# Head of an attention and mixing kernel: first third of q and k by halves of the heads, another load order, deeper load gates, a new order of operations with less padding

## The chip, the cores and the metric

The kernel runs on one core of one Trainium2 chip. The metric is the device time of one execution in microseconds (us), lower is better. The profile shows the core's span from first to last instruction, about 1.8 us shorter than the device time. The granted clock of TensorE is a share of full speed; it is 1.000 in the profiled run of the kernel before.

## The reference, cut to what matters

```python
# attention: q, k, v are [4, 8, 768, 64]; a token sees the first 8 tokens and the 96 before it
scores = scale * q @ k.T + bias                  # bias by head and distance
a = softmax(where(keep, scores, -1e9))
x = (a @ v), heads side by side                  # [4, 768, 512]
# then a mixing block
theta = x @ w_theta
zr, zi = x * cos(theta), x * sin(theta)
y = einsum('ts,bsd->btd', w_tok_r, zr) + einsum('ts,bsd->btd', w_tok_i, zi)
u = x + y
out = u + relu(u @ w_ch)
```

All arrays are float32; the kernel computes in bf16 with float32 accumulation.

## The kernel before

The program is a set of named operations and one list, ORDER, that gives the order in which they are written out. In the traces here each engine takes its own part of that list in order, so an operation that waits holds up those behind it on its engine (in a_256 below PE stands 1.93 us before a transpose, with the data of the scores behind it already there). Names carry batch, third of the sequence (256 tokens), and part: `t0010` transposes a k tile of batch 0 on TensorE (PE), `q000` and `k000` copy the result out of PSUM (the memory that matmuls write to), `kp` and `kg` make a second copy of k whose first 8 columns are the global tokens, `bi` writes the bias, `etab` makes a table of exponentials of it, `s` is one group of score matmuls (two heads), `x` the exponential, `v` the matmul with v, `n` the norm, `xt` the transpose of x (on PE in batches 0 and 1, by DMA in batches 2 and 3), `th` theta, `mx` the mixing, `ch` the last matmul, `load` and `gate` loads on GpSimd (POOL). "+27" behind a name asks for 27 padding matmuls on zeros before it.

```python
ORDER = """
... load4 sid3 etab6 bi0000
cast00/DVE bi0001 bi0010 etab3 load5 t0000 cast10/DVE bi0011 q000/DVE etab1 t0010+5 load6 k000/DVE etab2 kg000
kp000/DVE load7 etab0 cast01/DVE etab5 t0001+27 load8 cast11/DVE etab4 q001/DVE t0011+12 load9 k001/DVE kg001
s000+3 kp001/DVE load10 s001 x0000 x0001 load11 bi0020+3 t0100 ...
"""
```

The head loads q and k of the first 256 tokens of batch 0 as float32 over the queues of SP and ACT, one 128-token tile of all heads at a time, in runs of one token and head (64 floats, 256 B), and casts them on VectorE (DVE):

```python
a = new(st, "e", [T, H, D], FP)
(nc.sync, nc.scalar)[i].dma_start(out=a, in_=(q, k)[i][0, :, t * T:(t + 1) * T, :].rearrange("h p d -> p h d"))
...
vector[o.took](out=tiles[key][:, i, t].rearrange("p (h d) -> p h d", d=D), in_=tiles[st])
```

All other loads go through POOL and cast on the way. A load of number n, from the 20th on, is held by a gate, a one-element copy out of the landing place of load n - DEPTH:

```python
DEPTH = 5
add(f"gate{n}", {"POOL": 0.35},
    lambda: nc.gpsimd.tensor_copy(out=scrap, in_=landed[n - depth]()), ...)
...
ORD = 2     # third(1), v(0,0), v(0,1), third(2), v(0,2), then w_theta
```

The softmax here doesn't subtract the row's maximum and nothing guards it: scores larger than these inputs give would overflow.

Of the kernel before, what the change touches and what calls it, by code (L numbers as in the profile page):

```python
# [9 lines left out]
FP = mybir.dt.float32  # L10
# [27 lines left out]
ones6 hw00 hw10 zero rel ones3 tiny hw01 halfpi hw11 warm0 ones5 ones1 ones4 ones2 load1 ones0 ident sid0 far0  # L38
sid2 far1 load2 dtab0 dtab1 dtab2 load3 dtab3 sid4 sid5 etab7 sid1 sid6 sid7 load4 sid3 etab6 bi0000
cast00/DVE bi0001 bi0010 etab3 load5 t0000 cast10/DVE bi0011 q000/DVE etab1 t0010+5 load6 k000/DVE etab2 kg000  # L40
kp000/DVE load7 etab0 cast01/DVE etab5 t0001+27 load8 cast11/DVE etab4 q001/DVE t0011+12 load9 k001/DVE kg001
s000+3 kp001/DVE load10 s001 x0000 x0001 load11 bi0020+3 t0100 x0010 x0011 bi0021 bi0030 load12 q010/DVE t0110
bi0031 s003 k010/DVE load13 s002 x0030 kg010 kp010/DVE x0031 load14 vpa00/DVE x0020 vpb00/DVE x0021 bi0100+6
load15 v003 v000 v001 load16 bi0101 n000 s010 vpa01/DVE load17 bi0110 x0100 bi0111 vpb01/DVE s011 load18 x0101
n003 bi0120 v002 x0110 load19 n001 bi0121 s012 x0111 n002 bi0130 x0120 v010 bi0131 n010 s013 x0121 v011 x0130
v012 n011 t0200 x0131 n012 t0210 q020/ACT bi0200 k020/DVE xt00 bi0201 xc00/ACT bi0210 kp020/DVE bi0211 kg020
v013 vpa02/DVE s020 n013 s021 x0200 vpb02/DVE xt01+6 x0201 bi0220 gate20 x0210 xc01/DVE bi0221+1 load20 v020
x0211 s022 n020 tw00 gate21 x0220 v021 load21 twc00/DVE bi0230 x0221 bi0231 n021 s023 gate22 th000 x0230
load22 x0231 v022 tw10 ts0 gate23 n022 tw11 load23 v023 twc10/DVE th001 n023 gate24 twc11/ACT load24 tw01 xt02
cos000 twc01/DVE gate25 th011 sin000 load25 xc02/DVE cos001 z000 gate26 th010 load26 sin001 th020 z001 cos010  # L50
gate27 load27 sin010 th021 cos011 z010 gate28 t1000 sin011 load28 tw21 cos020 q100/DVE mx000 gate29 sin020
twc21/DVE load29 t1010 cos021 z011 gate30 mx010 sin021 k100/DVE load30 tx1 vpa10/DVE mx001 gate31 kg100 load31
vpb10/DVE z020 mx011 gate32 kp100/DVE load32 z021 tw20 s100 twc20/DVE s101 gate33 mx002 x1000 load33 x1001
x1010 mx012 u00 x1011 gate34 load34 s102 m101 s103 tw30 u01 x1020 gate35 mx020 x1021 m100 load35 x1030 m102
x1031 mx022 gate36 twc30/DVE load36 m103 mx021 gate37 load37 ut00 u02 ut01 uc00/ACT v102 gate38 t1110 uc01/DVE
load38 tw31 k110/DVE ch01 twc31/ACT gate39 kp110/DVE load39 t1100 kg110 o01 v101 v103 q110/DVE gate40 v100
st01 tw41 load40 ch00 n100 twc41/ACT n101 gate41 ut02 load41 tw40 vpa11/DVE uc02/ACT mx030 o00 twc40/ACT
gate42 vpb11/DVE load42 st00 mx032 n102 n103 mx031 gate43 load43 s110 gate44 u03 s111 load44 x1100 t1200 ch02
x1110 gate45 q120/DVE load45 x1101 ut03 x1111 t1210 m110 gate46 uc03/ACT s112 load46 m111 s113 k120/ACT mx040
o02 gate47 x1120 load47 mx041 kp120/DVE st02 x1121 kg120 gate48 x1130 tw51 m112 load48 v110 twc51/ACT tw50  # L60
n110 v111 mx042 gate49 x1131 n111 load49 twc50/ACT vpa12/DVE s120 u04 s121 gate50 x1200 mx050 load50 m113
x1210 vpb12/DVE ut04 x1201 gate51 ch03 uc04/DVE load51 x1211 m120 s122 o03 gate52 s123 x1220 mx051 load52 m121
x1230 st03 v113 x1221 gate53 xt10 n113 load53 x1231 mx052 m122 ts1 gate54 v120 load54 u05 v112 v121 v122 n112
xc10/ACT ut05 gate55 ch04 n120 load55 uc05/DVE th100 vpa20/DVE gate56 m123 load56 ch05 cos100 vpb20/DVE n121
gate57 sin100 v123 load57 xt11 n122 th101 n123 xc11/ACT gate58 load58 o04 xt12 cos101 o05 th110 st04 gate59
sin101 xc12/DVE load59 st05 th111 cos110 z100 gate60 sin110 th121 z101 load60 cos111 z110 th120 sin111 gate61
vpa21/DVE load61 z111 t2100 cos120 t2010 gate62 vpb21/DVE sin120 load62 t2000 q210/DVE cos121 mx110 z120
gate63 sin121 q200/DVE load63 mx111 k200/ACT z121 gate64 t2110 tx2 load64 kg200 mx112 kp200/DVE k210/DVE
gate65 s200 u11 load65 s201 mx100 x2000 kp210/DVE x2001 ut11 kg210 gate66 x2010 mx101 m200 load66 x2011 s202
m201 gate67 s203 t2200 vpa22/DVE load67 x2020 x2021 t2210 vpb22/DVE x2030 q220/DVE v200 gate68 mx102 x2031  # L70
load68 n200 k220/ACT s210 m203 gate69 s211 m202 load69 x2100 mx120 kp220/DVE x2101 u10 gate70 mx122 x2110
load70 m210 x2111 ut10 s212 kg220 gate71 v202 m211 v201 x2120 load71 ch11 n202 x2121 n201 gate72 v203 s213
load72 n203 mx140 x2130 m212 xt20 gate73 x2131 v210 load73 vpa30/DVE s220 n210 v211 x2200 mx121 gate74 n211
x2201 load74 vpb30/DVE s221 m220 s222 gate75 x2210 ch10 load75 u12 x2211 m213 v220 x2220 ut12 mx130 gate76
x2221 m221 load76 s223 n220 v221 gate77 x2230 m222 mx141 load77 x2231 n221 v222 ts2 gate78 v212 m223 mx131
load78 n212 v223 gate79 n222 v213 load79 mx132 n223 n213 gate80 th200 xt22 load80 o11 mx142 vpa31/DVE cos200
gate81 xt21 u13 load81 sin200 ch12 vpb31/DVE u14 gate82 th201 ut13 load82 o12 mx150 o10 cos201 ut14 z200
sin201 mx151 z201 st12 mx152 st11 th221 st10 u15 t3110 ut15 t3010 k310/DVE t3000 k300/DVE t3100 kp310/ACT
th211 q300/DVE q310/ACT kp300/DVE th210 kg300 kg310 vpa32/DVE th220 cos210 vpb32/DVE sin210 t3210 cos211 t3200
z210 ch13 k320/ACT q320/DVE mx200 sin211 kp320/DVE cos220 o13 ch14 sin220 z211 st13 cos221 mx210 z220 sin221  # L80
o14 mx201 tx3 z221 st14 s300 kg320 s301 mx202 x3000 x3010 mx212 x3001 u20 x3011 m300 s302 ut20 s303 m301 ch15
x3020 x3021 x3030 mx211 o15 x3031 s310 m303 st15 s311 u21 x3100 mx220 x3101 m302 ut21 v300 x3110 mx222 m310
x3111 n300 mx221 m311 v301 u22 v303 v302 v310 n302 ch20 ut22 n301 mx230 o20 n303 ch21 st20 n310 xt30 s312 o21
s313 x3120 mx232 x3121 st21 v311 x3130 mx231 n311 x3131 m312 s320 s321 u23 x3200 mx240 x3201 m313 ut23 v312
x3210 ch22 n312 x3211 m320 s322 s323 o22 x3220 mx241 x3230 m321 st22 v313 x3221 mx250 n313 x3231 m322 ts3 v321
xt31 v320 m323 mx252 n320 v322 v323 n321 ch23 n323 th300 n322 o23 xt32 mx242 cos300 sin300 th301 u24 st23 z300
th310 ut24 cos301 sin301 mx251 cos310 z301 th311 sin310 u25 mx300 z310 cos311 ut25 sin311 th320 z311 th321
cos320 sin320 mx301 cos321 z320 ch24 sin321 z321 mx310 o24 mx302 st24 mx312 u30 mx311 ut30 ch25 u31 mx320 ut31
o25 mx322 st25 mx321 ch30 u32 mx330 ut32 o30 mx331 st30 ch31 mx332 o31 mx340 st31 u33 mx341 ut33 mx342 ch32
u34 mx350 ut34 o32 mx352 st32 mx351 ch33 u35 ut35 o33 ch34 uc35/ACT st33 ch35 o34 ch351 o35 st34 o351 st35  # L90
st351
# [4 lines left out]
def kernel(  # L96
# [13 lines left out]
    nc = tc.nc  # L110
# [51 lines left out]
    DEPTH = 5  # L162
# [58 lines left out]
    def load(fn, us, ndesc, spot, depth=0, reads=(), writes=(), alloc=None):  # L221
        nload[0] += 1
        n = nload[0]
        landed[n] = spot
        after = [f"load{n - 1}"] if n > NFREE else ["hw00"]
        if n == NFREE + 1:
            after = [f"load{i}" for i in range(1, NFREE + 1)]
        if depth:
            add(f"gate{n}", {"POOL": 0.35},
                lambda: nc.gpsimd.tensor_copy(out=scrap, in_=landed[n - depth]()),  # L230
                reads=[("ld", n - depth)], prio=-100 + n - 0.5, after=after)
            after = [f"gate{n}"]
        add(f"load{n}", {"POOL": 0.62 + 0.00028 * ndesc}, fn, reads=reads, writes=list(writes) + [("ld", n)],
            alloc=alloc, prio=-100 + n if n > NFREE else None, lat=(1.05, us + {1: -0.12, 10: 1.1}.get(n, 0.0), 0.65), after=after)
# [39 lines left out]
    def first(i, t):  # L274
# [3 lines left out]
        def fn():  # L278
            a = new(st, "e", [T, H, D], FP)
            (nc.sync, nc.scalar)[i].dma_start(out=a, in_=(q, k)[i][0, :, t * T:(t + 1) * T, :].rearrange("h p d -> p h d"))  # L280

        add(f"hw{i}{t}", {eng: 0.5}, fn, writes=[st], alloc={st: "e"}, prio=-300 + t,
            lat=(0.9, (0.98, 0.7, 1.75, 0.88)[2 * t + i], 1.45), after=["hw00"] if i + t else [])

        def cast():
            if key not in tiles:
                new(key, "qk", [T, 2, 2, DM], BF)
            vector[o.took](out=tiles[key][:, i, t].rearrange("p (h d) -> p h d", d=D), in_=tiles[st])
# [12 lines left out]
    ORD = 2  # L301
# [436 lines left out]
```

## Time and profile before

| | before |
|---|---|
| device time | 174.28 us median of 3 (174.23 to 174.46) |
| span | 172.6 us, clock 1.000 |
| PE busy | 94% |
| first score matmuls | 10.02 us |
| last load issued by POOL | 100.41 us |

How to read it: PE is busy nearly all the time, so what counts is what it is busy with (padding is work of no use) and the few moments in which it waits. A useful mark in the timeline is the load of ACT's sine table, which comes after the last exponential of batch 0. The timeline's columns are start, duration, engine, line, operation and, in brackets, idle time before and what ended it:

```profile
28.30 1.28 ACT L673 ACT_TABLE_LOAD   x1
```

### The profile page before, as it was taken

How to read it: one execution, taken by the hardware profiler on the slowest of the kernel's cores; microseconds unless marked ns; L12 is line 12 of the kernel's file. 1: busy time of each engine (PE TensorE's matmuls, PEld its weight loads, DVE VectorE, ACT ScalarE, POOL GpSimd, SP SyncE). 2: the span in 40 equal slices, each digit the busy share in tenths (PEclk: the TensorE clock that was granted, in tenths of full speed). 3: DMA queues.
4: the chain of work that ended last, by engine and by line, in shares of the span. 5: the costliest groups of instructions: out<-in, count | busy, mean ns of one | idle time of the engine just before them, and what ended most of it. 6: DMA issues, size and time to landing. Idle time of an engine off the chain costs nothing.

```text
span 172.6 us, 4153 instructions
## 1 busy us (share of the span) xinstructions
PE 162.9 (94%) x1598; PEld 93.2 (54%) x1623; DVE 133.4 (77%) x315; ACT 106.0 (61%) x187; POOL 85.0 (49%) x150
## 2 busy tenths in 40 slices
PE   7998999999997999999999997999999999999991
PEld 2764776555664656565555643654555644444440
DVE  7948886798897698999999994795997975634442
ACT  3954988996445888799877540799518847300010
POOL 8998249779895899898996940000000000000000
PEclk9999999999999999999999999999999999999999
DMA  5999999999999999999999999612335364134334
GB/s 121 188 154 155 188 173 123 143 165 163 157 157 178 184 119 158 113 208 129 132 131 114 165 141 177 219 65 77 105 98 139 104 95 123 48 92 133 93 91 182
DMA packets 96868, 23.73 MB, mean 138 GB/s; under 512 B 91088, under 2 KB 93904, under 8 KB 96848
## 3 DMA queue, kind: packets, MB, share of 16 engines
q0 software_dynamic: 73504, 12.33, 100.7%
q1 hardware_dynamic: 21264, 10.62, 25.1%
q10 hardware_dynamic: 2080, 0.52, 1.7%
q8 instruction: 12, 0.20, 0.5%
q14 instruction: 8, 0.07, 0.1%
HBM read 25.69 MB, written 6.29 MB: 185 GB/s over the span
## 4 chain that ended last, share of the span: by engine, by line
PE 48%; DMA 30%; POOL 6%; DVE 6%; issue 5%; ACT 2%; DVEq 0%; POOLq 0%; SPq 0%; ACTq 0%
PE pb L592 22%; DMA qk<-in_k_dram 10%; PE pb L636 9%; PE pa L549 8%; DMA w_theta_bf<-in_moe_w_theta_dram 5%; DMA qk<-in_q_dram 4%; DMA xT<-x 4%; DMA uT<-u 3%; POOL qk L243 3%; DMA w_ch_bf<-in_moe_w_ch_dram 3%; PE pa L451 3%; PE pa L504 3%; PE pb L371 2%; POOL scrap L230 1%; DVE e L482 1%
## 5 line engine op out<-in xcount | busy, mean ns | idle before, releaser
L592 PE MATMUL pb<-zri,w_tokT 128*128 128x512 bf16 x273 | 67.3, 379 | 1.1 <-issue 0.5
L474 ACT ACTIVATE e<-pa 128x512 bf16<-128x512 f32 (+1 forms) x96 | 46.5, 565 | 20.0 <-PE pa L451 19.4
L592 PEld LDWEIGHTS <-w_tokT 128*128 128x128 bf16 x288 | 26.1, 98 | 28.2
L604 DVE TENSOR_TENSOR u<-x,pb 128x512 bf16<-128x512 bf16 x24 | 16.4, 682 | 11.9 <-PE pb L592 11.7
L636 PE MATMUL pb<-w_ch_bf,uT 128*128 128x512 bf16 (+1 forms) x96 | 24.0, 370 | 0.3
L549 PE MATMUL pa<-w_theta_bf,xT 128*128 128x512 bf16 x93 | 22.5, 379 | 1.3 <-DMA xT<-x 1.1
L482 DVE TENSOR_TENSOR e<-e,etab 128x1024 bf16<-128x1024 bf16 (+1 forms) x36 | 22.4, 639 | 0.4
L257 POOL DMA_DIRECT2D vn<-in_v_dram x24 | 21.8, 910 | 1.4 <-issue 1.4
L558 ACT ACTIVATE cs<-pa,halfpi 128x512 bf16<-128x512 f32 x24 | 16.6, 693 | 9.4 <-PE pa L549 9.2
L243 POOL DMA_DIRECT2D qk<-in_q_dram x22 | 19.6, 891 | 1.9 <-issue 0.9
L570 DVE TENSOR_TENSOR zri<-x,cs 128x1024 bf16<-128x1024 bf16 x24 | 16.2, 685 | 5.0 <-ACT cs L560 4.9
L243 POOL DMA_DIRECT2D qk<-in_k_dram x22 | 19.3, 877 | 0.0
L642 DVE SCALAR_TENSOR_TENSOR o<-pb,u 128x512 f32<-128x512 f32 (+1 forms) x25 | 16.2, 663 | 3.7 <-PE pb L636 3.7
L504 PEld LDWEIGHTS <-e 128*128 128x128 bf16 x352 | 14.5, 98 | 5.2
L517 DVE TENSOR_TENSOR x<-pa,rec 128x256 bf16<-128x256 f32 x36 | 15.3, 425 | 1.2
L620 ACT COPY uT<-pb 128x512 bf16<-128x512 bf16 x4 | 2.4, 594 | 20.9 <-PE pb L616 20.9
L549 PEld LDWEIGHTS <-xT 128*128 128x128 bf16 x96 | 8.9, 98 | 11.5 <-DMA xT<-x 1.6
L371 PE MATMUL pb<-ident,qk 128*128 128x128 bf16 x192 | 14.1, 221 | 1.0 <-DMA qk<-in_k_dram 1.0
L451 PEld LDWEIGHTS <-kk 64*128 64x128 bf16 x352 | 9.9, 94 | 9.3 <-issue 8.0
L451 PE MATMUL pa<-qT,kk 64*128 64x128 bf16 x352 | 14.9, 218 | 0.0
L560 ACT ACTIVATE cs<-pa 128x512 bf16<-128x512 f32 x24 | 14.4, 602 | 0.0
L230 POOL COPY scrap<-qk 1x1 bf16<-1x1 bf16 x33 | 11.3, 343 | 5.1 <-DMA qk<-in_k_dram 2.6
(69 smaller groups left out, 207.2 us busy)
## 6 DMA issues: line engine op xcount, KB each, us to landing
out_dram<-o SPq DMA_DIRECT2D x23, 256.0 KB, 2.3
vn<-in_v_dram POOLq DMA_DIRECT2D x24, 128.0 KB, 5.4
qk<-in_q_dram POOLq DMA_DIRECT2D x22, 128.0 KB, 5.5
qk<-in_k_dram POOLq DMA_DIRECT2D x22, 128.0 KB, 5.3
w_nat<-in_moe_w_tok_r_dram POOLq DMA_DIRECT2D x6, 192.0 KB, 6.0
w_nat<-in_moe_w_tok_i_dram POOLq DMA_DIRECT2D x6, 192.0 KB, 6.5
e<-in_k_dram ACTq DMA_DIRECT2D x2, 256.0 KB, 5.8
e<-in_q_dram SPq DMA_DIRECT2D x2, 256.0 KB, 5.1
```

The lines of the kernel that those rows point to most:

```text
L243: nc.gpsimd.dma_start(out=tiles[key][:, i, t].rearrange("p (h d) -> p h d", d=D), in_=(q, k)[i][b, :, r0:r0 + T, :].rearrange("h p d -> p ...
L257: nc.gpsimd.dma_start(out=v_bufs[i][:, t, :, 0:D], in_=v[b, :, r0:r0 + T, :].rearrange("h p d -> p h d"))
L371: nc.tensor.transpose(p_[:, t - u0, p], tiles[key][:, i, t, p * T:(p + 1) * T], ident)
L451: nc.tensor.matmul(p_[hh][:, s], lhsT=tiles["kk", b, kg][R, kt, p, r, :], rhs=tiles["qT", b, g][R, qt, p, :], start=not biased, stop=not b ...
L474: nc.scalar.activation(tiles[ek][:, hh, 0:n], tiles[pb[hh]][:, 0:n], AF.Exp, scale=scale)
L482: nc.vector.tensor_mul(e_[:, :, 0:n], e_[:, :, 0:n], etab[:, 2 * p:2 * p + 2, s0:s0 + n])
L504: nc.tensor.matmul(o, lhsT=l_, rhs=r_, start=(i == 0), stop=(i == len(mms) - 1))
L549: nc.tensor.matmul(p_, lhsT=tiles["xT", b, g][:, p, t, :], rhs=w_theta_bf[:, p, :], start=(p == 0), stop=(p == NP - 1))
L558: nc.scalar.activation(tiles[ck][:, 0], tiles[ps], AF.Sin, bias=halfpi)
L592: nc.tensor.matmul(p_, lhsT=w_tokT[wi][:, 2 * g + t, tt * T:(tt + 1) * T], rhs=tiles["z", b, g][:, t, wi, :], start=(n == 1 and t == 0 and ...
L604: nc.vector.tensor_add(u.rearrange("n (p c) -> n p c", p=NP), tiles["x", b, tt // 2][:, :, tt % 2, :], tiles[ps].rearrange("n (p c) -> n p ...
L636: nc.tensor.matmul(p_, lhsT=tiles["uT", b, tt][:, p, :], rhs=w_ch_bf[:, p, i * w:(i + 1) * w], start=(p == 0), stop=(p == NP - 1))
```

## The change

Its intent is to start the scores earlier and to hold PE up less. The transfers of the head bring four heads of both tiles instead of eight heads of one, in runs of two tokens (512 B), so that two of the four score groups can start after half the data. The later copy out of PSUM undoes the token order. Third 2 of q and k is loaded ahead of v of the middle third, and w_theta ahead of v of the last third. The gates are set to 8 loads in the first part and 6 later. The whole list of operations was ordered anew, with 24 padding matmuls where there were 63.

```diff
-    DEPTH = 5
+    DEPTH = 6
+    DEPTH1 = 8
...
-            a = new(st, "e", [T, H, D], FP)
-            (nc.sync, nc.scalar)[i].dma_start(out=a, in_=(q, k)[i][0, :, t * T:(t + 1) * T, :].rearrange("h p d -> p h d"))
+            a = new(st, "e", [T, H // 2, 2 * D], FP)
+            (nc.sync, nc.scalar)[i].dma_start(
+                out=a, in_=(q, k)[i][0, H // 2 * t:H // 2 * (t + 1), 0:2 * T, :].rearrange("h (p j) d -> p h (j d)", j=2))
...
+        third(1), load_v(0, 0), third(2), load_v(0, 1), load_w("w_theta", ...), load_v(0, 2)
...
+                vector[o.took](out=d_.rearrange("c t p (n j) -> c t p n j", j=2),
+                               in_=tiles[ps].rearrange("c p j (t n) -> c t p n j", t=2))
...
-kp000/DVE load7 etab0 cast01/DVE etab5 t0001+27 load8 cast11/DVE etab4 q001/DVE t0011+12 load9 k001/DVE kg001
-s000+3 kp001/DVE load10 s001 x0000 x0001 load11 bi0020+3 t0100 ...
+kp000/DVE t0001+17 kg000 cast11/DVE load7 etab2 s000 q001/DVE t0011 x0000 s001 load8 k001/ACT bi0020+1 x0001
+kp001/DVE load9 x0010 kg001 bi0021+3 t0100 ...
... (all further lines of ORDER, and code that is not reached, cut)
```

## The prediction

> **What bounds the kernel now.** I read, in this order: the busy shares and the 40 slices of the page, the waits of PE, the timeline of the first 36 us, the waits of POOL, and the chain that ended last.
>
> From the page, busy shares, then the slices:
> ```profile
> PE 162.9 (94%) x1598; PEld 93.2 (54%) x1623; DVE 133.4 (77%) x315; ACT 106.0 (61%) x187; POOL 85.0 (49%) x150
> ...
> PE   7998999999997999999999997999999999999991
> ...
> PEclk9999999999999999999999999999999999999999
> DMA  5999999999999999999999999612335364134334
> ```
> PE never rests for long and the clock is never throttled, so this is a kernel where PE's work, plus its few stalls, sets the time. The DMA engines are in use without a break until slice 26 (about 112 us), so a transfer issued before then competes with the loads.
>
> The waits of PE, all of them:
> ```profile
> PE pb L341 <- DVE zero L181: 1.2, 1, 1.2
> PE pa L549 <- DMA xT<-x: 1.1, 1, 1.1
> PE pb L371 <- DMA qk<-in_k_dram: 1.0, 1, 1.0
> PE pa L147 <- ACT e L474: 0.8, 2, 0.4
> PE pb L592 <- issue: 0.5, 3, 0.2
> ```
> Two single stalls stand out, each on a DMA: 1.0 us for a k tile (at 56.1 us in the timeline) and 1.1 us for a transposed x (at 106.4 us). The rest is small, but a busy PE need not be doing useful work. The timeline of the head shows what else it does:
> ```profile
> 6.73 1.55 PEld L145 LDWEIGHTS <-zero 128*128 128x128 bf16 x27
> ...
> 8.48 0.71 PEld L145 LDWEIGHTS <-zero 128*128 128x128 bf16 x12
> ...
> 10.02 0.51 PE L451 MATMUL pa<-qT,kk 64*128 64x128 bf16 x12
> ...
> 10.39 1.64 ACT L474 ACTIVATE e<-pa 128x384 bf16<-128x384 f32 x4 [1.07 <-PE pa L451]
> ...
> 13.43 1.64 ACT L474 ACTIVATE e<-pa 128x384 bf16<-128x384 f32 x4 [1.40 <-PE pa L451]
> ...
> 16.90 4.11 ACT L474 ACTIVATE e<-pa 128x512 bf16<-128x512 f32 x8 [1.83 <-PE pa L451]
> ```
> Lines 145 and 147 are padding matmuls on zeros that bridge time in which the data is not there. The first real scores run at 10.02 us and ACT idles 1.07 + 1.40 + 1.83 us between groups of exponentials: the head, not PE's throughput, is slack.
>
> The waits of POOL, which issues all loads but four:
> ```profile
> POOL scrap L230 <- DMA w_theta_bf<-in_moe_w_theta_dram: 3.6, 1, 3.6
> POOL scrap L230 <- DMA qk<-in_k_dram: 2.6, 4, 1.2
> POOL scrap L230 <- DMA qk<-in_q_dram: 2.3, 4, 1.2
> ```
> Line 230 is the gate: load n waits until load n-5 has landed. These waits are about 10 us in sum with the smaller ones. The chain that ended last confirms who set the stall at 106 us:
> ```profile
> 99.09 7.33 DMA xT<-x
> 106.42 0.05 issue
> ```
>
> **What the Trainium skill says.** "DMA: Bandwidth & Descriptors", Specifications, gives 512 B as the least transfer for line rate, and the section Why small descriptors are slow puts a fixed cost on each packet. The trace agrees: the four head transfers move 256 B pieces, 4,100 packets and 1.05 MB between about 2.65 and 7.35 us, so about 223 GB/s; rows of w_theta (2 KB of f32 read, 1 KB of bf16 written) reach about 205 GB/s counted on the written side, about 410 read. "TensorE: Matmul & The Clock Gate", Back-to-back issue gap, gives N/2.4 + 2.5 ns for a warm matmul, so 56, 162 and 216 ns for 128, 384 and 512 columns; the trace agrees (27 weight loads of padding in 1.55 us, 57 ns each; ten of line 549 in 2.16 us). The same page's section on the HAM clock gate says about 3.4 us of work warms the array; here the matmuls of the warm-up start 0.43 us apart until 4.6 us. "DMA: Bandwidth & Descriptors", Issuing engines are not separate DMA queues, says all queues share 16 engines: DMA transposes of x took 6.7 to 7.3 us from issue to landing while loads ran and 3.0 to 3.4 us after 110 us.
>
> **The change part by part.**
>
> 1. *Head by halves.* Before, each head transfer brings one 128-token tile of all eight heads; scores need both tiles of q and k, so all four. After, each brings four heads of both tiles, in 512 B runs: 2,048 packets instead of 4,096 for the same bytes. Scores of heads 0 to 3 need only the first q and the first k transfer. Landings before: 4.75, 5.43, 7.47, 8.07 us. With 512 B I estimate 300 GB/s (between 223 and 410), so 3.5 us instead of 4.7: the last lands near 7.0. The first cast gains little: DVE is busy with the preamble until 5.15 us. After it: two casts 1.12 us (to 6.2), q copy about 0.65 (its PSUM read is now permuted, so I take it slower than the 0.42 us measured), k copy on ACT meanwhile, cast 0.56, second copy of k 0.35 and its small one 0.15: first scores at about 7.8 us instead of 10.0. Cost: four permuted copies, 0.2 us each, two of them on ACT. ACT can take it, because the etab exponentials now interleave with the first score exponentials instead of all eight (5.12 us) running first.
>
> 2. *Padding.* Before: 44 + 6 of 128 columns x 56 ns = 2.80, 6 of 384 x 162 = 0.97, 7 of 512 x 216 = 1.51 (the trace lost one): 5.3 us. After: 17 x 56 = 0.95, 4 x 162 = 0.65, 3 x 216 = 0.65: 2.25 us. PE's list is 78 rows shorter, 39 matmuls with their loads, and all real work is unchanged. If PE's stalls do not grow, this is worth **3.0 us** directly, since PE runs almost unbroken from the head to the end. The earlier start of the scores is what permits it; it is not a second gain.
>
> 3. *Load order.* Third 2 of q and k moves to loads 7-10 (before 9-12), v of the middle third to 11-12, w_theta to 13 (before 15), v of the last third to 14-15. Landings of loads 7-10 in the old run were 14.0 to 18.1 us, load 12 at 19.9; about 1.2 us less for the shorter head gives 16.5 to 17 for the last k, 18.7 for v, then w_theta (2.5 us at the old rate) at about 21. Counting PE's real work, the first theta comes after 18.4 us of it, plus 1.2 us start and 2 to 3 us of stalls: 22. It fits, with little to spare; v of the middle third fits by about 2 us, the transposes of the last k hardly.
>
> 4. *Depth.* In the first part of the loads the gate goes from 5 to 8. The ninth load on POOL, which has no gate, already waits for the first landing (idle 0.36 at 9.09 us), so eight seem to be in flight at most and the gate becomes free. Load 20 could issue near 20 us rather than 24.1. Later the depth is 6. POOL then has less to wait (some 10 us in sum before), so the last load should be issued at 92 to 97 us instead of 100.4. That helps both stalls: the k at 56 us comes earlier, and the x transposes near 100 us meet fewer loads. PE also asks earlier (by 3 us), so I count half of the 2.1 us: **1.0 us**.
>
> 5. *New order everywhere.* The order of all operations is new. Between issue and use of a DMA transpose in batch 2 there are 5.2, 4.8 and 4.3 us of PE work (before 8.1, 7.0 and 5.2), against 7 us latency under loads: this only fits if the loads end sooner. For ACT the head gets dense: etab 5.1 + exponentials 11.5 + copies 1.9 from 4.2 us gives 22.7 before the sine table, against 28.3 in the old trace; PE's last values of batch 0 would wait for that about 1 us. For this and the tight arrivals I add **0.4 us** net.
>
> Sum: 174.28 - 3.0 - 1.0 + 0.4 = 170.7 us.
>
> **The rivals.**
>
> *Data does not keep up.* Padding was there because PE waited; take it out and PE may simply idle until the same bytes land. For it: DMA is full until 112 us, and the total bytes do not change. Against: the head packets halve, and between 26 and 30 us the loads ran at about 1,000 packets per us against 1,220 earlier, so gates, not the engines, limited them. It would leave 172.5 to 174 us.
>
> *A late DMA transpose becomes the bound.* The three short distances of point 5, all in batch 2. For it: 6.7 to 7.3 us latency. Against: loads end earlier. Two new stalls of 1 to 1.5 us each would make it 172.5 to 173.
>
> *Everything fits and both old stalls vanish.* PE's remaining work after the first scores is 1.1 us less than before (padding after that point 2.4 to 1.3 us), and scores start 2.2 us earlier; both stalls go too: 168.9 us.
>
> **Range and chances.** The padding is counted, not guessed, so the sign is nearly sure; the stalls can add or take 1.5 to 2 us. Range 168.8 to 173.0. The 2% line is 170.8, almost at my middle: faster 0.50, same 0.48, slower 0.02.
>
> **What would show it.** The first scores near 7.8 us, not 10. Exponentials with gaps under 1 us each before the sine table, and that table load near 23 us. Lines of padding with 24 matmuls. POOL's waits on gates well under 10 us and its last load before 97 us. PE's list of waits without the two single 1 us stalls. The prediction is wrong if PE waits on DMA for qk, vn or xT by more than 2 us in sum, if the first scores stay above 9 us, or if the clock drops in the head for want of padding.

## More of the kernel before

A score group writes two of four PSUM buffers that theta and the values of later batches use as well. Its matmuls contract over 64 rows; the two heads of a group sit in the lower and upper 64 rows:

```python
for s, (kg, kt, r, qt) in enumerate(slots):
    for hh in range(2):
        R = slice(D * hh, D * (hh + 1))
        nc.tensor.matmul(p_[hh][:, s], lhsT=tiles["kk", b, kg][R, kt, p, r, :], rhs=tiles["qT", b, g][R, qt, p, :], ...)
```

## The result

The changed kernel takes 172.19 us (median of 4 fast runs, 172.06 to 172.32) against 174.28 us for the kernel before (median of 3 fast runs; a fourth took 177.04 us, over 1.5% above the fastest, and counts as slow). A ratio here is always the mean time of one kernel's fast runs over the mean of the other's fast runs of the same rounds, so it is not quite the ratio of the medians that are quoted. It is 0.9878, 95% interval 0.9858 to 0.9897: faster, by less than 2%. The clock was 1.000.

The page of the changed kernel, busy shares and the DMA slices:

```profile
PE 162.4 (95%) x1559; PEld 91.0 (53%) x1584; DVE 134.8 (79%) x319; ACT 101.8 (60%) x183; POOL 83.1 (49%) x150
...
DMA  4999999999999999999999349510644534143334
```

There are 39 matmuls fewer, and the loads are through three slices (some 13 us) earlier. All waits of PE in the changed kernel:

```profile
PE pb L355 <- DVE zero L185: 1.2, 1, 1.2
PE pa L147 <- ACT e L526: 0.6, 1, 0.6
PE pb L644 <- issue: 0.5, 3, 0.2
PE pa L499 <- DVE qT L436: 0.3, 1, 0.3
PE pb L688 <- issue: 0.3, 2, 0.2
```

Both single stalls on a DMA are gone. A new wait, on a copy of q, has come. POOL's largest waits have shrunk as well:

```profile
POOL scrap L234 <- DMA vn<-in_v_dram: 1.3, 2, 0.7
POOL scrap L234 <- DMA w_theta_bf<-in_moe_w_theta_dram: 1.1, 1, 1.1
```

The head in the timeline of the changed kernel, PE, then ACT's mark:

```profile
8.13 0.34 PE L499 MATMUL pa<-qT,kk 64*128 64x128 bf16 x6
8.40 0.40 PE L418 MATMUL pb<-ident,qk 128*128 128x128 bf16 x4
8.73 0.23 PE L499 MATMUL pa<-qT,kk 64*128 64x128 bf16 x2
9.28 0.29 PE L499 MATMUL pa<-qT,kk 64*128 64x128 bf16 x4 [0.32 <-DVE qT L436]
...
10.65 0.65 PE L147 MATMUL pa<-zero 128*128 128x384 bf16 x3 [0.65 <-ACT e L526]
```

```profile
25.42 1.28 ACT L733 ACT_TABLE_LOAD   x1
```

The first scores run at 8.13 us instead of 10.02 and the sine table is loaded 2.9 us earlier. But the second score group stops after two of its six matmuls until a copy on DVE is done:

```profile
8.54 0.69 DVE L436 COPY qT<-pb 128x512 bf16<-128x512 bf16 x1 [0.33 <-PE pa L499]
```

To see where the gain arises I added up PE's useful matmuls in both traces, each at its undisturbed spacing (216 ns for 512 columns, 56 for 128, 30 for 65, 28 for a score matmul, and so on). I counted them by their weight loads, one for each matmul, since those records are complete in both traces (the matmuls' own are not), and noted the time at which equal amounts of useful work were done:

| useful PE work done | before, at us | changed, at us | difference |
|---|---|---|---|
| 14 us (late in batch 0's attention) | 27.53 | 25.80 | -1.73 |
| 40 us | 54.16 | 53.19 | -0.97 |
| 45 us (after the old stall on k) | 60.80 | 58.28 | -2.52 |
| 85 us | 102.80 | 101.70 | -1.10 |
| 90 us (after the old stall on x) | 109.11 | 106.70 | -2.41 |
| 145 us | 165.39 | 163.18 | -2.21 |

A weight load can start some tenths ahead of its matmul, so a row is uncertain by that much. The head gives 1.7 us. Around the two lost stalls the difference grows by 1.6 and 1.3 us, somewhat more than the waits of 1.0 and 1.1 us. In the other stretches the changed kernel gives 2.4 us back, a little at a time, without any wait in its list. The experiments look for the 1.3 us that the head fell short of the predicted 3.0, and for this slow loss.

### The profile page after: what moved, and what is told of

The parts are those of the page before. It is cut to its first block, busy times and chain, and to the rows that moved or that the text cites. A ratio compares the mean times of both kernels' runs of the same rounds, so it can differ in the third digit from the quotient of the medians.

```text
span 170.4 us, 4072 instructions
## 1 busy us (share of the span) xinstructions
PE 162.4 (95%) x1559; PEld 91.0 (53%) x1584; DVE 134.8 (79%) x319; ACT 101.8 (60%) x183; POOL 83.1 (49%) x150
## 3 DMA queue, kind: packets, MB, share of 16 engines
q1 hardware_dynamic: 20240, 10.62, 25.4%
## 4 chain that ended last, share of the span: by engine, by line
PE 90%; ACT 3%; DVE 2%; issue 2%; DVEq 0%
PE pb L644 33%; PE pa L601 12%; PE pb L688 12%; PE pa L499 8%; PE pb L425 6%; PE pa L556 5%; PE pa L490 3%; PE pb L367 3%; PE pb L355 2%; PE pb L556 2%; PE pb L582 2%; PE pb L668 1%; PE pa L147 1%; ACT e L526 1%; ACT L713 1%
## 5 line engine op out<-in xcount | busy, mean ns | idle before, releaser
L526 ACT ACTIVATE e<-pa 128x512 bf16<-128x512 f32 (+1 forms) x96 | 47.6, 564 | 22.4 <-PE pa L499 22.2
L601 PE MATMUL pa<-w_theta_bf,xT 128*128 128x512 bf16 x91 | 23.1, 379 | 0.2
L499 PE MATMUL pa<-qT,kk 64*128 64x128 bf16 x352 | 17.2, 219 | 0.5 <-DVE qT L436 0.3
L688 PEld LDWEIGHTS <-uT 128*128 128x128 bf16 x100 | 8.9, 98 | 8.6 <-ACT uT L672 0.3
L425 PE MATMUL pb<-ident,qk 128*128 128x128 bf16 x176 | 13.0, 219 | 0.0
```

What stands on the lines that cost most here:

```text
L425: nc.tensor.transpose(p_[:, t - u0, p], tiles[key][:, i, t, p * T:(p + 1) * T], ident)
L526: nc.scalar.activation(tiles[ek][:, hh, 0:n], tiles[pb[hh]][:, 0:n], AF.Exp, scale=scale)
L601: nc.tensor.matmul(p_, lhsT=tiles["xT", b, g][:, p, t, :], rhs=w_theta_bf[:, p, :], start=(p == 0), stop=(p == NP - 1))
L688: nc.tensor.matmul(p_, lhsT=tiles["uT", b, tt][:, p, :], rhs=w_ch_bf[:, p, i * w:(i + 1) * w], start=(p == 0), stop=(p == NP - 1))
```

## The experiments

Each kernel was timed in five rounds against the kernel before, on three chips: chip 2 (b_nopad, a_nopad, b_split, a_merge), chip 5 (a_depth5, a_ord2, a_256, a_s001) and chip 11 (a_merge5, a_s001_nopad, a_all, b_nopad_again). The median of the kernel before was 174.6 to 175.2 us there, but its runs scatter more (172.6 to 177.7 us), so the intervals of the ratios are about half a per cent to either side. The changed kernel was not timed again in these rounds. So a comparison with its 172.19 us crosses rounds and is less sure than the marks in the traces, or than two variants on one chip. All results were correct.

The medians in the table are over all runs, slow ones too. Without the slow runs b_nopad has 172.80 us and b_split 177.80.

| run | median us | ratio to before (95%) |
|---|---|---|
| changed kernel | 172.19 | 0.9878 (0.9858 to 0.9897) |
| b_nopad | 173.21 | 0.9884 (0.9826 to 0.9942) |
| b_nopad_again | 172.69 | 0.9894 (0.9829 to 0.9960) |
| a_nopad | 171.46 | 0.9819 (0.9766 to 0.9872) |
| b_split | 177.91 | 1.0143 (1.0078 to 1.0209) |
| a_merge | 174.94 | 1.0006 (0.9960 to 1.0051) |
| a_merge5 | 172.88 | 0.9910 (0.9856 to 0.9964) |
| a_depth5 | 175.87 | 1.0101 (1.0046 to 1.0156) |
| a_ord2 | 172.54 | 0.9911 (0.9867 to 0.9954) |
| a_256 | 173.38 | 0.9969 (0.9916 to 1.0022) |
| a_s001 | 171.19 | 0.9834 (0.9792 to 0.9877) |
| a_s001_nopad | 171.40 | 0.9824 (0.9750 to 0.9897) |
| a_all | 171.81 | 0.9862 (0.9788 to 0.9936) |

### The kernel before without padding (b_nopad, b_nopad_again)

```diff
-... t0001+27 ... t0011+12 ... s000+3 ...
+... t0001 ... t0011 ... s000 ...      (all "+n" removed, 63 padding matmuls)
```

> The kernel before without any of its 63 padding matmuls (5.3 us of PE time), nothing else touched. Theory 1 (padding only fills time in which PE would wait for data, so removing it turns it into waits): ratio 0.995 to 1.005 of before, PE idle in the head grows by what the padding took. Theory 2 (as the prediction counted it: padding stands on PE's path and its removal is a direct gain): 3 to 5 us faster, ratio 0.97 to 0.983. Theory 3 (padding keeps the clock up): slower, and a clock under 1.0 in the first 30 us.

One of six runs, the profiled one, took 569.67 us. PE ran there at about a quarter of its speed from the first warm-up matmul on, ahead of any place where padding had been. The other five took 171.54 to 173.73 us at clocks of 0.980 to 0.987.

> The kernel before without padding once more, because the profiled run of the first time fell into a state in which PE ran at about a quarter of its speed from its first matmul on, so it has no usable trace. If that state came from the missing padding: it shows again in one run of six or so, or the clock is under 1.0 in several. If it was chance: all runs near 172.8 us, ratio 0.985 to 0.992, and the trace shows about 3 us more idle time of PE in the head than before (5.1 us of padding less, 2 us of time less).

All six runs took 171.77 to 173.31 us, at clocks of 0.975 to 0.990; the quarter speed did not come again. The sine table was loaded at 28.54 us, against 28.30 with the padding. So the head gained nothing at all from 5.3 us of padding less. The busy time by stretches (columns: stretch, length, busy PE, PEld, DVE, ACT, POOL, clock, DMA share, GB/s) shows one reason:

```profile
6.00:9.00 3.00, 1.18 (x10) 0.59 (x10) 2.80 (x8) 3.00 (x6) 2.70 (x4) 0.86 2.09 167
9.00:12.00 3.00, 2.56 (x25) 1.76 (x26) 1.09 (x4) 1.87 (x5) 2.77 (x4) 0.50 2.46 155
12.00:15.00 3.00, 2.87 (x26) 1.95 (x25) 1.86 (x5) 0.48 (x3) 3.00 (x4) 0.50 2.43 155
```

Without padding PE is busy only 1.18 us between 6 and 9 us, the granted clock falls to half at 8.18 us and comes back at 15.01 us. The padding before had filled waits and had kept the clock up. The kernel without it is faster all the same, by 1.1%, but it gains later: its sine table of batch 0 is 0.24 us later than before and its exponential table of batch 3 is 1.34 us earlier. Its list of PE's waits shows neither of the two old stalls, on k or on x, although its gates and its order are those of before. Why they went when only padding was removed I did not settle. Of the three theories, the clock of theory 3 came true, but not its slower time.

### The changed kernel without padding (a_nopad)

> The changed kernel without its 24 padding matmuls (2.2 us of PE time). Theory 1 (padding fills waits): ratio to before stays 0.985 to 0.990, as for the changed kernel (0.988). Theory 2 (padding on the path): 1.5 to 2.2 us faster still, ratio 0.975 to 0.979. Theory 3 (clock): slower than the changed kernel, ratio above 0.992.

The four runs at clocks of 0.997 to 1.000 took 171.06 to 171.81 us, the two at 0.989 and 0.990 took 173.05 and 172.19. The sine table came at 24.50 us instead of 25.42. Of the 2.2 us of padding 0.9 us was on the path, the rest had filled waits, and some executions pay with the clock. The truth lies between theory 1 and theory 2.

### The second score group ahead of the copy (a_s001)

```diff
-... s000 q001/DVE t0011 x0000 s001 load8 k001/ACT ...
+... s000 s001 q001/DVE t0011 x0000 load8 k001/ACT ...
```

> The changed kernel with the second score group placed ahead of the copy of the second q half, nothing else. In the trace its matmuls stop for 0.54 us until that copy is done, though they do not read what it writes. Theory W (that wait is on PE's path in the head): 0.3 to 0.6 us faster than the changed kernel, ratio 0.984 to 0.987. Rival (the next wait, for the exponentials that free score buffers, takes it over): within 0.2 us, ratio 0.987 to 0.989.

All runs lie between 171.03 and 171.54 us, 1.0 us under the changed kernel and more than expected; on the same chip a_ord2, which has the old place of the group, took 172.28 to 172.97. The sine table came at 24.56 us. PE's timeline has the two groups in one piece:

```profile
7.93 0.51 PE L499 MATMUL pa<-qT,kk 64*128 64x128 bf16 x12
```

Theory W holds. In the changed kernel the copy `q001` writes columns of the last four heads in both token tiles, and the group `s001` reads columns of heads 2 and 3. They share no element, but the range that the copy spans, from tile 0 to tile 1, encloses what the last four matmuls read in tile 1; just these four waited. That the dependency was drawn from the range is my reading of this pattern; no run shows the bookkeeping. What followed was a chain: group late, exponential late behind a k copy on ACT, PE waiting 0.65 us for the buffer.

### Both head edits, and the candidate (a_s001_nopad, a_all)

> The changed kernel with both head edits that helped alone: the second score group ahead of the copy of the second q half (1.0 us) and no padding (1.1 us, or less since on another chip). If the two are separate waits on PE's path they add: about 2 us under the changed kernel, ratio to before 0.974 to 0.979. If both shorten the same chain (the exponentials of the head then set the pace): only 1.0 to 1.4 us, ratio 0.979 to 0.983.

The table came at 23.92 us, where 25.42 - 0.86 - 0.92 would give 23.64: in the trace the two add nearly. In time they do not: three runs at clocks of 0.997 to 1.000 took 170.39 to 170.81 us, three at 0.990 took 171.99 to 172.41. Without padding the clock drops in some executions, and that eats the gain.

> The candidate: second score group early, no padding, five pairs of score groups together. If the three effects add: about 3.2 us under the changed kernel, 169 us, ratio to before 0.967 to 0.973. If the head edits overlap: 170 us, ratio 0.972 to 0.978. If pairing does nothing: as without pairs, 0.974 to 0.983.

With the five pairs that a_merge5 below tests on top it is 171.81 us. On the same chip and at clocks of 0.997 to 1.000 its runs took 171.32 to 171.98 us, those without pairs 170.39 to 170.81, so pairing took away rather than gave. The best steady version is a_s001, whose runs all lie below those of both kernels; a_s001_nopad has the fastest single run.

### Pulling score groups apart (b_split)

```diff
-... s100 twc20/DVE s101 gate33 mx002 ...
+... s100 twc20/DVE gate33 mx002 s101 ...      (13 such pairs in batches 1 to 3)
```

> The kernel before with 13 of its pairs of score groups in batches 1 to 3 pulled apart: the second group of each pair is placed one matmul group (0.86 us) later, so PE enters and leaves the scores 33 times there instead of 20; the work is the same. Theory F (each entry into and exit from the 64-row score matmuls costs PE about 0.27 us, read from the start-to-start gaps around them): 13 x 0.27 = 3.5 us slower, ratio 1.015 to 1.022. Rival (the gaps at the borders are only latency that the neighbours hide, and the late idle time of the changed kernel has other causes): ratio 0.997 to 1.006.

It is 1.4% slower, 2.5 us: a loss, as theory F says, but less than its 3.5 us. The timeline of PE before, around one pair, then of b_split:

```profile
39.28 0.51 PE L451 MATMUL pa<-qT,kk 64*128 64x128 bf16 x12
39.73 1.90 PE L592 MATMUL pb<-zri,w_tokT 128*128 128x512 bf16 x8
```

```profile
41.23 0.34 PE L451 MATMUL pa<-qT,kk 64*128 64x128 bf16 x6
41.50 1.04 PE L592 MATMUL pb<-zri,w_tokT 128*128 128x512 bf16 x4
```

Twelve score matmuls hold PE for 0.45 us until the next mixing matmul starts, six hold it for 0.27 us: not half. Measured with the entry, from the start of the last mixing matmul before to the first one after, less the 216 ns of that one, the visits that nothing else disturbs take 369 ns for 6 matmuls, 425 for 8, 538 for 12 and 649 for 16, in the traces of before, after and b_split. Two visits of 8 cost 850 ns, one of 16 costs 649: **each further visit costs 0.20 us**, the matmuls themselves 28 ns each. Thirteen more visits make 2.6 us, next to the 2.5 measured (1.4 to 3.7 by the interval). Two cautions: two of the seven runs were slow ones and are left out of the ratio; and the profiled run, the slowest of the fast ones, is 5.1 us longer than before by its span, since PE also waited longer there, for k tiles above all (2.4 us instead of 1.0). So the total alone would not fix the price of a visit; the spacing does.

"TensorEngine Tiling (Array Packing)" of the Trainium skill, section Key Properties, says that changing the tiling mode drains TensorE. The score matmuls use 64 rows, their neighbours 128, so each visit changes it twice; the trace agrees with a cost at the border and gives its size.

The changed kernel visits the scores 28 times in batches 1 to 3, the kernel before 20 times. Eight more visits are 1.6 us by this measure: two thirds of the slow loss of 2.4 us in the table of useful work. The rest stays open.

### Bringing score groups together (a_merge, a_merge5)

```diff
-... s100 mx011 gate33 ... mx001 tx1 gate34 z021 load34 s101 ...
+... mx011 gate33 ... mx001 tx1 gate34 z021 load34 s100 s101 ...   (ten pairs; five in a_merge5)
```

> The changed kernel with score groups of batches 1 and 2 brought together in pairs, 20 entries into the scores in batches 1 to 3 instead of 28 (before has 20); the exponentials that stood between move behind the pair, all else stays. Theory F (0.27 us for each entry and exit): 8 x 0.27 = 2.2 us faster than the changed kernel, ratio to before 0.972 to 0.980. Rival 1 (no cost at the borders): 0.985 to 0.992. Rival 2 (pairs take all four score buffers and PE then waits for exponentials): slower than the changed kernel, above 0.992, with new waits of PE on ACT.

With ten pairs the gain did not come; it is 2.7 us slower than the changed kernel by the medians, 2.2 by the ratios. The waits of PE say why:

```profile
PE pa L499 <- ACT e L526: 1.2, 2, 0.6
PE pa L556 <- ACT e L526: 0.9, 2, 0.5
PE pb L688 <- DMA uT<-u: 0.8, 1, 0.8
```

Two groups in a row fill all four buffers, and the second, or the values behind it, wait for exponentials. Rival 2 is what happened.

> The changed kernel with only five pairs of score groups brought together, those that in the run with ten pairs showed no wait between or behind them: 23 entries into the scores in batches 1 to 3 instead of 28. Theory F (about 0.24 us of PE for each entry and exit, as the trace with the split pairs shows): 5 x 0.24 = 1.2 us faster than the changed kernel, ratio to before 0.980 to 0.984. Rival (the borders are absorbed elsewhere): 0.986 to 0.990. A third outcome, slower with PE waiting for exponentials between the pairs, would say that pairing itself costs here.

This miss is partly mine: the five pairs leave 25 visits, not the 23 that I wrote, because two of the moves only exchange partners. Three visits less should give 0.6 us; a wait of 0.6 us between the groups of one pair (on an exponential again) took it. That would leave the time as it was, but the span is 0.6 us longer than the changed kernel's, which I did not explain. So the border cost is measured, but I have no version in which saving visits pays: here a pair brings a buffer wait of at least the same size.

### The old gates (a_depth5)

```diff
-    DEPTH = 6
-    DEPTH1 = 8
+    DEPTH = 5
+    DEPTH1 = 5
```

> The changed kernel with the gate back at 5 loads everywhere (instead of 8 in the first part and 6 later). Theory D (the deeper gate is what removed the two 1 us stalls of PE on a k tile and on a transposed x): POOL waits about 10 us at gates again, the last load is issued near 100 us and not 88, one or both stalls come back, ratio to before 0.993 to 1.003 (changed kernel 0.988). Rival (the new order of operations alone removed them): 0.985 to 0.990 and no PE wait on a DMA over 0.5 us.

It is 1% slower than the kernel before and 3.7 us slower than the changed one (174.76 to 176.58 us against 172.06 to 172.32; a_ord2 on the same chip took 172.28 to 172.97). This is the largest effect of all. The last load is issued at 98.95 us instead of 88.27. The sine table of batch 0 comes at 25.38 us as in the changed kernel, so nothing is lost in the head; the loss begins with batch 1. The waits of DVE, then of PE:

```profile
DVE vp L457 <- DMA vn<-in_v_dram: 3.1, 3, 1.3
```

```profile
PE pa L499 <- DVE x L569: 0.9, 1, 0.9
```

A copy on DVE that waits for v (1.3 us the longest time) holds the norms and copies behind it, and PE then waits for those. The changed kernel has no wait of DVE on a DMA. Theory D is right that the gate carries the later part, but what comes back are waits on v and not the two old stalls: that the deeper gates removed those is not shown. The run sets both depths back at once, so it doesn't tell which of them counts. The new order of operations asks for data earlier and needs the deeper gates: with the old ones it is slower than the old order.

### The old load order (a_ord2)

```diff
-    ORD = 5
+    ORD = 2
```

> The changed kernel with the loads of batch 0 in the old order (v of two thirds before q and k of the last third, w_theta after the last v), the order of operations unchanged. Theory L (the early transposes of the last third live from the new load order): q lands with load 11 instead of 9, k with load 12 instead of 10, 1.5 to 2 us later, PE waits for them in the head, 1 to 2 us slower than the changed kernel, ratio 0.993 to 1.000. Rival (other waits, of ACT's exponentials, hide it): 0.985 to 0.990.

The runs lie between 172.28 and 172.97 us, 0.35 us over the changed kernel by the medians. The intervals of the ratios overlap, so it is not clear of noise. The rival holds: the load order is worth little.

### Halves by heads with 256 B pieces (a_256)

```diff
-            (nc.sync, nc.scalar)[i].dma_start(out=a, in_=... "h (p j) d -> p h (j d)" ...)
+            for j in range(2):
+                (nc.sync, nc.scalar)[i].dma_start(out=a[:, :, j * D:(j + 1) * D],
+                    in_=(q, k)[i][0, H // 2 * t:H // 2 * (t + 1), j * T:(j + 1) * T, :].rearrange("h p d -> p h d"))
```

> The changed kernel with the halves by heads kept, but each half moved as two transfers of 256 B pieces with tokens in plain order (eight head transfers instead of four, 4,096 packets instead of 2,048; the copies out of PSUM are then not permuted). Theory P (the packet size is what makes the head land early): the four halves land 0.5 to 1 us later each, first scores at 8.6 to 9.2 us instead of 8.1, 0.5 to 1 us slower than the changed kernel, ratio 0.991 to 0.994. Rival (halving by heads is what counts, and DVE's preamble and chain set the first scores; the plain copies of 0.42 us even repay the later landing): 0.985 to 0.990.

The halves landed at 4.83, 5.36, 8.65 and 8.99 us, against 4.55, 5.00, 6.13 and 6.96 in the changed kernel, and the first scores ran at 10.03 us, although their own data was late by only 0.4 us: PE stood 1.93 us before a transpose of the second q half, which stands ahead of them in its list:

```profile
9.70 0.40 PE L420 MATMUL pb<-ident,qk 128*128 128x128 bf16 x4 [1.93 <-DVE qk L295]
```

Three runs at full clock took 172.92 to 172.95 us, 0.7 us over the changed kernel; three in which the clock fell (0.987 to 0.989) took 173.81 to 174.82. The trace is of the slowest of these: its clock was at half for 3.41 us from 11.44 us on, after the landings and the first scores. Theory P is right in direction. But eight transfers are also issued later than four (the last at 2.43 us instead of 1.26), so I cannot part the packet size from the number of transfers.

## Why the prediction was right or wrong

The time was within the range and the direction right; the gain was 2.1 us where 3.6 was forecast. That the total came this near is partly luck, since errors cancelled: 1.3 us too much for the padding, 1.1 too little for the stalls, 1.2 too little for the cost of the new order.

**Point 1, the head by halves,** was right. The last landing was forecast near 7.0 us and came at 6.96, the first scores were forecast at 7.8 us and came at 8.13. The permuted copy took 0.67 to 0.69 us on DVE, as assumed. One reading in it was off, though: the SP queue's pieces flow from 1.88 us on, not from 2.65, so the old rate was 192 GB/s and not 223; with 512 B it was 245 GB/s (1.85 to 6.12 us) and not 300. The two errors cancelled: the movement got 1.2 us shorter in both accounts.

**Point 2, the padding, is the step that failed.** It took 3.0 us of padding as a direct gain "if PE's stalls do not grow". But for 3.0 us of padding less the head is only 1.7 us shorter by the table of useful work: the other 1.3 us turned into waits and wider spacing. In the kernel before, padding was not simply on the path: without any of it the head is as long as with it, and the clock falls. In the changed kernel 0.9 of 2.2 us was on the path. The 1.7 us came mainly with data that arrives earlier: with the same little padding but later data (a_256) the sine table comes at 27.98 us, next to 28.30 before, though a clock at half is part of that. The false wait of the second score group stopped 0.9 us more by the same mark, which a_s001 recovers.

**Point 3, the load order,** was right that it fits: w_theta landed at 20.4 us, and the first theta ran only at 24.0, 2 us later than forecast. a_ord2 shows that the order hardly matters.

**Point 4, the depth,** was too small, and its mechanism is shown only in part. Both old stalls went, 2.1 us and not 1.0, and the last load was issued at 88.3 us, earlier than the 92 to 97 forecast. The new order needs the deeper gates (a_depth5), but they need not be what removed the stalls: with the old gates these did not come back, and in b_nopad_again, with the old gates and the old order, they are missing too. Transposes of x then took 3.0, 3.3 and 4.4 us from issue to landing in batch 2, where they had taken 6.7 to 7.3.

**Point 5, the new order,** was too small: 0.4 us. It cost up to 2.4 us, the slow loss. Eight more visits to the scores at 0.20 us are 1.6 us, a cost that I had not looked for, though the short gaps were in the trace of before. The sine table was forecast near 23 us and came at 25.4, because ACT still stood 2.4 us in gaps before its copies and exponentials; the sum of its work was right.

The account by the runs: -1.7 (head) - 2.1 (stalls) + 1.6 (visits) = -2.2 us, and the span is 2.2 us shorter. That it closes so well is partly chance: in the table of useful work the stretches with the stalls give 2.9 us and the slow loss is 2.4.

**The rivals.** "Data does not keep up" did not happen with the new gates and did with the old ones (waits of DVE on v, 3.1 us). Between 26 and 30 us the loads of the kernel before ran at 907 packets per us, somewhat under the 1,000 that the prediction read; its point stands. "A late DMA transpose becomes the bound" did not happen. "Everything fits" came true for both stalls, but its 168.9 us knew nothing of the borders and of the false wait.

## What to carry to other kernels

Padding is neither free nor simply time to be won: before counting it as a gain, find what PE would wait for in its place, and what the clock does without it. An operation that shares a tile with a strided write can be held although no element is shared; place it ahead of the write. When a list is reordered, count how often PE changes between 64-row and 128-row matmuls, since each visit had a fixed price here (0.20 us), and set the depth of the load gates anew, because an order that asks for data earlier can lose all its gain to them (here 3.7 us).

## What the Trainium skill lacked or had wrong

- "TensorEngine Tiling (Array Packing)", Key Properties, says that a change of the tiling mode drains TensorE but gives no size. Here one visit to 64-row matmuls among 128-row ones costs 0.20 us beyond the matmuls (649 ns for one visit of 16, 850 for two of 8).
- "TensorE: Matmul & The Clock Gate", the part on the HAM clock gate, gives in its table one idle window of about 3.4 us as what makes the clock fall and about 3.4 us of work as what brings it back (further down it tells of a kernel that idled briefly and often enough to make the clock swing, without a figure). In b_nopad_again it fell at 8.18 us although PE was never idle for more than 1.6 us, and came back only after 6.83 us, with PE busy 2.56 and 2.87 us of each 3 us. In a_256 it fell at 11.44 us, with no idle time over 1.93 us, and came back after 3.41 us, as the page says.
- The same page reports a gate stuck at a quarter for over 50 us, and that the records can't be trusted. Here a whole execution of 569.67 us ran at about a quarter of the speed, from the first matmul on; its trace holds no clock record at all, and the summary gave 1.000. It came in one of the twelve runs of this kernel.
- No page that I read gives the time of a DMA transpose beside other loads: here 5 to 7 us from issue to landing while loads run, 2.4 to 3.4 us for most after them.
